# Attention with two gated layers on one core: the planner's transfer rate set to 290 GB/s instead of 265, and all work ordered anew

## The chip, the core and the metric

The kernel runs on one core of a Trainium2 chip. A core has five instruction queues: PE (TensorE, matmuls and transposes; its weight loads are listed as PEld), DVE (VectorE), ACT (ScalarE), POOL (GpSimd) and SP (SyncE), which here issues all the transfers between memory and the on-chip buffers. Each engine works through its own instructions strictly in order and waits on semaphores for what others have to deliver. The metric is device time in microseconds (us), the median of several executions. The profile is of one execution.

## The reference, cut to what matters

```
scores = q @ k.T / 8                       # 4 batches, 8 heads, 576 tokens, head size 64
keep, in each row of 576, the 32 largest; softmax over them; out = attn @ v
x = out as [2304 tokens, 512]
x = (silu(x @ wg) * (x @ wv)) @ wo         # first gated layer, width 1536
x = (sigmoid(x @ wg2) * (x @ wv2)) @ wo2   # second gated layer, other weights
```

All of it in float32. The weights arrive from the host as 64-bit words.

## The kernel before, in words

**Chunks.** The 2304 tokens (36 tiles of 64) are cut into six chunks of 4, 5, 6, 7, 7 and 7 tiles, called chunk 0 to chunk 5. For each chunk the program states attention first and then both layers.

**Attention.** For a pair tile (two times 64 query rows of two heads) PE makes scores in PSUM (`ps_s`, L685 or L668), ACT copies them to `s` (L695, L702; four buffers). DVE finds the 32nd largest of each row with four MAX8 (L875) and three MATCH_REPLACE (L877) for each half of the tile. ACT then makes the exponentials (L835, L839), a reciprocal is taken on DVE (L850), the row is normed into `p` on POOL or ACT (L857, L855), PE transposes it (`ps_t`, L917), ACT copies it to `pt` (L923) and PE multiplies with `v` (`ps_v`, L936).

**Weights.** There are 36 slabs of weights, each of two halves. In chunk 0 each of the 72 halves is loaded as 64-bit words into `wr` (512 KB, three buffers), decoded to float32 by three operations on ACT and POOL (L518 or L520, L532, L541 or L543) and a fourth on DVE (`f4`, L546), which writes the buffer `wf`. From `wf` PE multiplies at once in float32 (L977, operands `xn` and `hn`), and SP stores `wf` to memory as `sw` (256 KB, L550). The chunks 1 to 5 load `sw` again into `raw` (256 KB), split it into a high and a low part (`w`: L498 or L500 for the high one, L503 on POOL for the low one) and do three matmuls for one.

**Layers.** A block of the first product is one `ps_m` tile: four matmuls in chunk 0, twelve in the others. ACT takes the tanh (L1012), DVE multiplies (L948, L952), ACT and POOL split the result into `hh` and `hl`.

**Early scores.** Eight pair tiles of chunk 5 are scored while chunk 0 runs, into `se`, and stored to memory as `ss` (L624). They are loaded again much later (L815).

**What sets the order.** Nothing is issued as stated above. Every piece of work is an `op` with an engine, or a choice of engines, a planned length, what it depends on, which buffers it takes, and a priority. `Plan.run` plays the work through on planned times: whenever an engine is free it takes the ready op of the lowest priority number, and the order in which ops were taken becomes the order of instructions on every engine. A transfer is planned as if one line carried them all, one after another, for `n_bytes / 265.0` ns each, and its data are there 2010 ns (`DMA_LAT`) later. The numbers in the tables at the head of the file (`P_...`, `D_...`, `N...`, one number for each chunk or one for all) are the priorities: `D_WR` of the `wr` loads, `D_ST` of the `sw` stores, `D_RAW` of the `raw` loads, `P_ROUND` of the search for the 32nd largest. `E_SKIP`, `E_IN` and `E_STEP` say between which other ops the early scores are stated.

Of the kernel before, what the change touches and what calls it, by code (L numbers as in the profile page):

```python
# [11 lines left out]
I32 = mybir.dt.int32  # L12
# [5 lines left out]
ALU = mybir.AluOpType  # L18

P = 128  # L20
# [20 lines left out]
EARLY = '000002'  # L41
E_FIRST = 0
E_STEP = 1
E_SKIP = 3
E_LAST = 1
E_IN = [0, 0, 0, 0, 0, 0]
WR = 3
E_PRIO = 0
E_DMA = 2.5
WU = 3  # L50
KE = 2
HP = 3
DL = 6
NA = [0, 2, 2, 2, 2.5, 3]
NP = [1, 1, 0, 0, 2, 0]
P_XC = [0, 1, 0.5, 1, 0, 1]
P_EV = [1, 1, 1, 1, 1, 1]
D_WR = 13
D_ST = 5
D_RAW = [6, 4, 1.0, 2.5, 2.0, 2.5]  # L60
D_K = [0, 1, 1, 3, 0, 1]
D_V = [2.5, 0.5, 4.5, 2.5, 1.5, 2.5]
P_ROUND = [4, 4, 6, 4, 4, 2]
P_MASK = [3, 2, 2, 2, 1, 1]
P_DEC = 2
P_MM = [5, 4.5, 7, 5.5, 6, 6]
P_QK = [0, 1, 3.5, 1.5, 1.0, 3.5]
P_K = [1, 1, 1, 1.5, 1, 5]
P_PT = [2.5, 3.5, 2.5, 2.5, 2.5, 5.5]
P_PV = [1, 1, 0, 2, 0, 0]  # L70
P_EX = [1.5, 3.5, 1.5, 1.5, 0, 0]
P_S = [0.5, 0, 1, 0, 0, 0]
P_X = [1, 0.5, 0, 0, 1.5, 0]
P_HH = [0.5, 1, 2.5, 0.5, 1.0, 2.0]
P_HL = [2, 1.5, 0, 2, 4, 2]
PT = 1
WF = 16
XF = 8
# [15 lines left out]
DEBUG = False  # L94
F1 = {"act": (609, 2), "pool": (700, 2)}
F2 = {"act": (609, 2)}
F3 = {"act": (650, 2), "pool": (810, 2)}
LO = 0
TURN = 2
# [34 lines left out]
class Plan:  # L134
# [5 lines left out]
    def op(self, eng, dur, fn, deps=(), uses=(), allocs=(), prio=0, table=None, lat=DMA_LAT, lock=False):  # L140
        o = Op()
        o.lock = lock
        o.alts = dict(eng) if isinstance(eng, dict) else {eng: (dur, prio)}
        o.eng, o.fn, o.table, o.lat = None, fn, table, lat
        o.deps = [d for d in deps if d is not None]
        o.uses = list(uses) + list(allocs)
        o.allocs = list(allocs)
        o.seq = len(self.ops)
        for g in o.uses:
            g.users += 1  # L150
        self.ops.append(o)
        return o
# [165 lines left out]
def dve(n):  # L318
    return 69 + n / 0.96
# [12 lines left out]


def dma(n_bytes):
    return n_bytes / 265.0


@with_exitstack
def attn_moe_kernel(ctx: ExitStack, tc, qT, kT, qD, kD, vL, wall, outT):
    nc = tc.nc  # L340
    ctx.enter_context(tc.manual_schedule())
    plan = Plan()
    op = plan.op
# [166 lines left out]
    def decode(i, x, prio):  # L510
        r, f, u = new(("wr", 0)), new(("wf", 0)), new(("wu", 0))
        ld = load(r, wall[2 * i + x].bitcast(I32).rearrange("p (a b) -> p a b", b=2),
                  n_bytes=128 * 4096, prio=D_WR)
# [28 lines left out]
            else:  # L542
                nc.gpsimd.tensor_scalar(o, b, 1.0 / 32, -31.0 / 64, op0=ALU.mult, op1=ALU.add)  # L543

        def f4():
            nc.vector.scalar_tensor_tensor(out=f[:].bitcast(I32), in0=f[:].bitcast(I32), scalar=3, in1=u[:],  # L546
                                           op0=ALU.logical_shift_left, op1=ALU.bitwise_or)

        def st():
            nc.sync.dma_start(scr32[i][:, x], f[:])  # L550
        a = op(F1, 0, f1, deps=[ld], uses=[r], allocs=[f])
        b = op(F2, 0, sign, deps=[ld], uses=[r], allocs=[u])
        d = op(F3, 0, f3, deps=[ld], uses=[r], allocs=[u])
        b = op("dve", dve(512) + 30, f4, deps=[a, b, d], uses=[f, u], prio=prio, lock=True)
        stored[i].append(op("dma", dma(128 * 2048), st, deps=[b], uses=[f], prio=D_ST, lat=DMA_LAT))
        return f, b

# [204 lines left out]
    def segment(c, p, b, q0, n_s, x32g, col, held=None):  # L762
# [55 lines left out]
    def row_tile(sg, stg, a, e, pg):  # L818
# [341 lines left out]
```

## Time and profile before

| | us |
|---|---|
| median of 3 runs | 1262.02 |
| lowest and highest of them | 1261.18, 1265.14 |
| the profiled execution, its own time | 1263.24 |
| its span, first to last instruction | 1261.5 |
| PE busy | 1214.4 |
| DVE busy | 881.5 |
| ACT busy | 871.3 |
| POOL busy | 963.9 |

Busy time of PE is the time in which it has at least one matmul under way; ends of matmuls are modelled, so two starts that follow each other tell more than a duration. In the table of stretches below, a row has the stretch in us from the span's start, its length, the busy time of each engine with the number of its instructions in brackets, the granted clock of TensorE as a share of 2.4 GHz, the mean busy share of the 16 DMA engines, and the rate that they moved in GB/s.

### The profile page before, as it was taken

How to read it: one execution, taken by the hardware profiler on the slowest of the kernel's cores; microseconds unless marked ns; L12 is line 12 of the kernel's file. 1: busy time of each engine (PE TensorE's matmuls, PEld its weight loads, DVE VectorE, ACT ScalarE, POOL GpSimd, SP SyncE). 2: the span in 40 equal slices, each digit the busy share in tenths (PEclk: the TensorE clock that was granted, in tenths of full speed). 3: DMA queues.
4: the chain of work that ended last, by engine and by line, in shares of the span. 5: the costliest groups of instructions: out<-in, count | busy, mean ns of one | idle time of the engine just before them, and what ended most of it. 6: DMA issues, size and time to landing. Idle time of an engine off the chain costs nothing.

```text
span 1261.5 us, 21915 instructions
## 1 busy us (share of the span) xinstructions
PE 1214.4 (96%) x7304; PEld 1064.8 (84%) x7304; DVE 881.5 (70%) x1916; ACT 871.3 (69%) x1906; POOL 963.9 (76%) x1030
## 2 busy tenths in 40 slices
PE   5699999989999999999999999999999999999998
PEld 1366867778999899999999898999888899999998
DVE  7999999983999989889989799931949310121110
ACT  5789888876999898788999886344877532332331
POOL 3434455569999999989897887898796587897883
PEclk9699999999999999999999999999999999999999
DMA  7877887876554464544554456335232232433331
GB/s 245 267 249 256 259 267 253 260 260 200 156 170 129 130 197 125 160 138 134 158 156 133 128 178 188 122 101 170 73 111 68 85 104 97 146 117 113 104 104 43
DMA packets 100914, 200.38 MB, mean 159 GB/s; under 512 B 12480, under 2 KB 22848, under 8 KB 100800
## 3 DMA queue, kind: packets, MB, share of 16 engines
q1 hardware_dynamic: 100800, 198.98, 49.5%
q8 instruction: 57, 0.93, 0.3%
q14 instruction: 57, 0.47, 0.1%
HBM read 171.21 MB, written 27.72 MB: 158 GB/s over the span
## 4 chain that ended last, share of the span: by engine, by line
PE 62%; DVE 11%; ACT 4%; DMA 3%; POOL 2%; issue 1%; SPq 0%; POOLq 0%; ACTq 0%; DVEq 0%
PE ps_m L977 52%; DVE st L875 5%; DVE wk L877 4%; PE ps_v L936 4%; PE ps_t L917 3%; PE ps_s L668 3%; DMA wr<-in_wall_dram 1%; DMA raw<-sw 1%; POOL w L503 1%; ACT w L498 1%; ACT p L839 1%; ACT e L835 1%; DVE h L948 1%; ACT s L695 0%; DVE wf L546 0%
## 5 line engine op out<-in xcount | busy, mean ns | idle before, releaser
L503 POOL TENSOR_TENSOR w<-raw,w 128x512 fp32r<-128x512 f32 x360 | 465.4, 1310 | 10.5 <-ACT w L498 3.3
L977 PE MATMUL ps_m<-xh,w 128*128 128x448 f32 (+2 forms) x1920 | 398.4, 349 | 0.3 <-DVE sil L948 0.3
L977 PEld LDWEIGHTS ps_m<-xh,w 128*128 128x128 f32 x1920 | 336.6, 188 | 16.2 <-issue 1.3
L875 DVE MAX8 st<-wk 128x8 f32<-128x576 f32 x432 | 315.0, 748 | 1.0
L977 PE MATMUL ps_m<-xl,w 128*128 128x448 f32 (+2 forms) x960 | 215.6, 346 | 0.0
L877 DVE MATCH_REPLACE8 wk<-st,wk 128x576 f32<-128x576 f32 x288 | 213.1, 742 | 0.0
L977 PE MATMUL ps_m<-hh,w 128*128 128x448 f32 (+2 forms) x960 | 200.5, 350 | 0.0
L977 PEld LDWEIGHTS ps_m<-xl,w 128*128 128x128 f32 x960 | 172.1, 188 | 7.1
L977 PEld LDWEIGHTS ps_m<-hh,w 128*128 128x128 f32 x960 | 168.8, 188 | 8.1
L498 ACT ACTIVATE w<-raw 128x512 fp32r<-128x512 f32 x249 | 151.5, 624 | 20.5 <-PE ps_m L977 8.4
L503 POOL TENSOR_TENSOR hl<-h,hh 128x448 fp32r<-128x448 f32 (+2 forms) x120 | 128.7, 1074 | 8.3 <-ACT hh L498 5.1
L875 DVE MAX8 st<-s 128x8 f32<-128x576 f32 x144 | 105.1, 747 | 32.3 <-ACT s L695 31.7
L948 DVE SCALAR_TENSOR_TENSOR sil<-sil,ps_m 128x448 f32<-128x448 f32 (+3 forms) x84 | 41.0, 489 | 123.1 <-ACT sil L1012 123.0
L498 ACT ACTIVATE hh<-h 128x448 fp32r<-128x448 f32 (+2 forms) x113 | 61.1, 542 | 93.2 <-DVE h L948 66.3
L835 ACT ACTIVATE e<-s,st 128x576 f32<-128x576 f32 x144 | 109.8, 769 | 16.5 <-DVE st L875 15.6
L923 ACT ACTIVATE pt<-ps_t 128x512 f32<-128x512 f32 (+4 forms) x288 | 112.8, 418 | 11.2 <-PE ps_t L917 9.7
L917 PE MATMUL ps_t<-ident,p 128*128 128x128 f32 x656 | 102.6, 283 | 14.8 <-POOL p L857 6.6
L948 DVE SCALAR_TENSOR_TENSOR h<-sil,ps_m 128x448 f32<-128x448 f32 (+2 forms) x60 | 34.4, 574 | 117.0 <-PE ps_m L977 113.5
L500 POOL TENSOR_SCALAR w<-raw 128x512 fp32r<-128x512 f32 x111 | 69.2, 625 | 57.1 <-PE ps_m L977 56.3
L917 PEld LDWEIGHTS ps_t<-ident,p 128*128 128x128 f32 x656 | 77.8, 143 | 40.8 <-POOL p L857 14.3
L839 ACT ACTIVATE p<-e,st 128x576 f32<-128x576 f32 x144 | 110.4, 768 | 1.7 <-PE ps_t L917 0.8
L1012 ACT ACTIVATE sil<-ps_m 128x448 f32<-128x448 f32 (+4 forms) x156 | 71.7, 459 | 56.7 <-PE ps_m L977 56.2
(64 smaller groups left out, 1812.3 us busy)
## 6 DMA issues: line engine op xcount, KB each, us to landing
raw<-sw SPq DMA_DIRECT2D x360, 256.0 KB, 3.0
wr<-in_wall_dram SPq DMA_DIRECT2D x72, 512.0 KB, 4.6
sw<-wf SPq DMA_DIRECT2D x72, 256.0 KB, 2.7
kr<-in_kD_dram SPq DMA_DIRECT2D x42, 288.0 KB, 3.0
v<-in_vL_dram SPq DMA_DIRECT2D x34, 320.0 KB, 3.9
ss<-se SPq DMA_DIRECT2D x6, 576.0 KB, 2.9
s<-ss SPq DMA_DIRECT2D x6, 576.0 KB, 5.2
k<-in_kT_dram SPq DMA_DIRECT2D x11, 288.0 KB, 4.4
```

What stands on the lines that cost most here:

```text
L498: nc.scalar.activation(out=hi(), in_=raw(), func=AF.Copy)
L500: nc.gpsimd.tensor_scalar(hi(), raw(), 1.0, 1.0, op0=ALU.mult, op1=ALU.mult)
L503: (nc.gpsimd if eng == "pool" else nc.vector).tensor_sub(lo(), (lo_raw or raw)(), lo_hi() if lo_hi else f32(hi()))
L835: nc.scalar.activation(out=eg[:], in_=src(), func=AF.Prelu, bias=stg[:, 31:32], scale=-1.0, alpha=1.0 / STEEP)
L839: nc.scalar.activation(out=pg[:, e * S:(e + 1) * S], in_=eg[:], func=AF.Exp, bias=stg[:, 32:33], scale=-STEEP, accum_out=stg[:, 33:34])
L875: nc.vector.max(out=stg[:, 4 * k:4 * k + 8], in_=src() if k == 0 else fresh[:])
L877: nc.vector.match_replace(out=fresh[:], in_to_replace=stg[:, 4 * k - 4:4 * k + 4], in_values=src() if k == 1 else fresh[:], imm_value=NEG)
L917: nc.tensor.transpose(tg[:width, i], pg[:, a:a + width], ident)
L923: nc.scalar.activation(out=dst(), in_=src(), func=AF.Copy)
L948: nc.vector.scalar_tensor_tensor(out=out, in0=t, scalar=1.0, in1=x, op0=ALU.add, op1=ALU.mult)
L977: nc.tensor.matmul(pg[:, :n], blk(a, d), src(x, d), start=first and i == 0, stop=last and i == 4 * len(terms) - 1)
L1012: nc.scalar.activation(out=sg[:, :n], in_=pg[:, :n], func=AF.Tanh, scale=0.5)
```

## The change

The planned rate of a transfer goes from 265 to 290 GB/s, and 17 of the constants and tables at the head are set to other numbers. Two of them move where the early scores are stated: they now begin inside chunk 0's attention. `f4` gets a table of engines of its own; it names DVE alone, with the same length and priority as before, so the branch for POOL in it is never taken. A small tile `eight` is filled once by POOL.

```diff
-E_SKIP = 3
+E_SKIP = 4
-E_IN = [0, 0, 0, 0, 0, 0]
+E_IN = [2, 0, 2, 0, 0, 0]
...
-D_WR = 13
-D_ST = 5
+D_WR = 12.5
+D_ST = 4
...
+F4 = {"dve": (632, 2)}
...
 def dma(n_bytes):
-    return n_bytes / 265.0
+    return n_bytes / 290.0
...
+    eight = pool("eight", 1).tile([P, 1], I32, tag="eight", name="eight")
+    nc.gpsimd.memset(eight, 8)
...
-        def f4():
+        def f4(eng):
...
-        b = op("dve", dve(512) + 30, f4, deps=[a, b, d], uses=[f, u], prio=prio, lock=True)
+        b = op(F4, 0, f4, deps=[a, b, d], uses=[f, u], lock=True)
```

The same instructions remain, apart from the choice between ACT and POOL for some of them; the order of all five queues is new. Lines stand up to seven further down in the changed file: L491 is L494 there, L546 is L551, L550 is L557, L624 is L631, and behind these all are seven further (L875 is L882, L977 is L984). A number at the end of a name is only the order in which buffers were made.

First place: DVE, behind the 55th of the 72 decodes and up to the 57th (`wf` is a decode; `st`, `wk` and `s` belong to the search). Before:

```order
L877 MATCH_REPLACE wk_2477<-st_2468,wk_2477 128x576
L877 MATCH_REPLACE wk_2509<-st_2473,wk_2509 128x576
L875 MAX st_2468<-wk_2477 128x8
L875 MAX st_2473<-wk_2509 128x8
L546 SCALAR_TENSOR_TENSOR wf_2556<-wf_2556,wu_334 128x512
L877 MATCH_REPLACE wk_2509<-st_2473,wk_2509 128x576
L875 MAX st_2592<-s_2223 128x8
L875 MAX st_2473<-wk_2509 128x8
L850 RECIPROCAL st_2468<-st_2468 128x1
L877 MATCH_REPLACE wk_2607<-st_2592,s_2223 128x576
L948 SCALAR_TENSOR_TENSOR hn_2244<-sil_2596,ps_m_2586 128x256
L546 SCALAR_TENSOR_TENSOR wf_2594<-wf_2594,wu_355 128x512
```

In the changed kernel, the same two decodes:

```order
L882 MAX st_2353<-wk_2372 128x8
L882 MAX st_2446<-s_2161 128x8
L884 MATCH_REPLACE wk_2372<-st_2353,wk_2372 128x576
L884 MATCH_REPLACE wk_2458<-st_2446,s_2161 128x576
L955 SCALAR_TENSOR_TENSOR hn_2185<-sil_2448,ps_m_2437 128x256
L551 SCALAR_TENSOR_TENSOR wf_2444<-wf_2444,wu_319 128x512
L551 SCALAR_TENSOR_TENSOR wf_2462<-wf_2462,wu_351 128x512
```

Eight instructions of the search stood before these two decodes, and four stand there now. Ahead of the last decode there are 166 MAX, 124 MATCH_REPLACE and 40 reciprocals in the order before, and 153, 114 and 36 in the new one.

Second place: SP, the first stores of early scores (`ss`) among loads (`wr`, `v`) and stores of weights (`sw`). Before:

```order
L550 DMA sw_67<-wf_688 128x512
L491 DMA wr_750<-in_wall_dram 128x1024
L624 DMA ss_0_2_195<-se_734 128x1152
L550 DMA sw_68<-wf_722 128x512
L550 DMA sw_68<-wf_740 128x512
L624 DMA ss_0_4_196<-se_784 128x1152
```

In the changed kernel:

```order
L494 DMA wr_462<-in_wall_dram 128x1024
L557 DMA sw_65<-wf_449 128x512
L631 DMA ss_0_2_200<-se_464 128x1152
L494 DMA v_520<-in_vL_dram 128x640
L494 DMA wr_530<-in_wall_dram 128x1024
L631 DMA ss_0_4_201<-se_517 128x1152
```

The first store stood behind the 15th load of `wr` and now stands behind the 8th. All eight such stores now stand ahead of the 19th load of `wr`, where before it was four.

Third place: PE, where chunk 0 ends and chunk 1 begins (`hn`,`wf`: chunk 0; `xh`, `xl`, `w`: chunk 1). Before:

```order
L917 MATMUL ps_t_3050<-ident,p_2967 128x128
L977 MATMUL ps_m_3025<-hn_2244,wf_3021 128x256 x4
L977 MATMUL ps_m_3025<-hn_2244,wf_3047 128x256 x4
L917 MATMUL ps_t_3091<-ident,p_3057 128x128 x4
L977 MATMUL ps_m_3099<-xh_1882,w_3064 128x320 x4
L977 MATMUL ps_m_3099<-xh_1882,w_3066 128x320 x4
L977 MATMUL ps_m_3099<-xl_1883,w_3064 128x320 x4
L977 MATMUL ps_m_3127<-xh_1882,w_3065 128x320 x4
L977 MATMUL ps_m_3127<-xh_1882,w_3067 128x320 x4
L977 MATMUL ps_m_3127<-xl_1883,w_3065 128x320 x4
```

In the changed kernel:

```order
L984 MATMUL ps_m_3035<-hn_2185,wf_2891 128x256 x4
L984 MATMUL ps_m_3075<-xh_1924,w_2904 128x320 x4
L984 MATMUL ps_m_3075<-xh_1924,w_2906 128x320 x4
L984 MATMUL ps_m_3075<-xl_1925,w_2904 128x320 x4
L984 MATMUL ps_m_3104<-xh_1924,w_2905 128x320 x4
L984 MATMUL ps_m_3104<-xh_1924,w_2907 128x320 x4
L984 MATMUL ps_m_3104<-xl_1925,w_2905 128x320 x4
L924 MATMUL ps_t_3129<-ident,p_3093 128x128 x4
L984 MATMUL ps_m_3035<-hn_2185,wf_2937 128x256 x4
L924 MATMUL ps_t_3184<-ident,p_3093 128x128 x4
L924 MATMUL ps_t_3193<-ident,p_3093 128x128
```

The four matmuls on the last decoded half (`wf_3047`, now `wf_2937`) stood ahead of chunk 1's first block. Two blocks of chunk 1 now stand ahead of them.

## Rows read from the trace of the kernel before

**Rows 1.** The page, busy time of PE over the span.
```profile
PE 1214.4 (96%) x7304; PEld 1064.8 (84%) x7304; DVE 881.5 (70%) x1916; ACT 871.3 (69%) x1906; POOL 963.9 (76%) x1030
```

**Rows 2.** Busy time by stretch; columns as told above.
```profile
32.00:256.00 224.00, 204.00 (x1447) 147.86 (x1446) 221.91 (x499) 193.18 (x427) 106.74 (x155) 0.93 0.80 260
256.00:320.00 64.00, 58.79 (x348) 51.65 (x347) 40.13 (x85) 45.13 (x95) 51.88 (x53) 0.97 0.70 222
320.00:559.00 239.00, 236.96 (x1585) 222.20 (x1584) 221.47 (x493) 211.28 (x493) 223.53 (x219) 1.00 0.49 150
```

**Rows 3.** The chain that ended last, two long pieces: start us, us, what.
```profile
241.08 4.68 DMA wr<-in_wall_dram
...
997.14 174.27 PE ps_m L977 x867
```

**Rows 4.** Longest wait of DVE in 32 to 256 us: sum, times, longest.
```profile
DVE wf L546 <- ACT wu L532: 0.6, 1, 0.6
```

**Rows 5.** DVE in order of time, 214 to 236 us: start us, us, what.
```profile
213.92 1.39 DVE L875 MAX8 st<-s 128x8 f32<-128x576 f32 x2
215.24 0.07 DVE L877 MATCH_VALUE_LOAD wk<-st,s 128x8 f32 x1
...
217.56 0.07 DVE L877 MATCH_VALUE_LOAD wk<-st,s 128x8 f32 x1
...
218.28 0.07 DVE L877 MATCH_VALUE_LOAD wk<-st,wk 128x8 f32 x1
...
220.28 0.14 DVE L850 RECIPROCAL st<-st 128x1 f32<-128x1 f32 x1
220.34 0.73 DVE L875 MAX8 st<-wk 128x8 f32<-128x576 f32 x1
```

**Rows 6.** Tile wr, 120 to 276 us: count, ns min/median/max, first and last start.
```profile
L491 SPq DMA_DIRECT2D wr<-in_wall_dram x46: 327/358/1903, 119.7 to 268.1; - x46
L543 POOL TENSOR_SCALAR wu<-wr x41: 770/782/1337, 121.9 to 273.7; 128x512 uint8<-128x512 uint8 x41
L520 POOL TENSOR_SCALAR wf<-wr x29: 651/670/1266, 125.9 to 273.0; 128x512 f32<-128x512 f32 x29
...
DMA to landing us min/median/max: 3.5/4.5/6.6
```

**Rows 7.** The 32 us with the most moved between 64 and 256 us.
```profile
160.00:192.00 32.00, 31.14 (x183) 21.89 (x177) 31.91 (x69) 28.23 (x64) 19.21 (x26) 1.00 0.85 267
```

**Rows 8.** The 8 us with the most moved in that stretch.
```profile
112.00:120.00 8.00, 7.03 (x73) 5.05 (x76) 8.00 (x19) 7.59 (x19) 3.86 (x5) 1.00 0.90 304
```

**Rows 9.** Tile wf, 120 to 276 us, its decodes on DVE; columns as for tile wr.
```profile
L546 DVE SCALAR_TENSOR_TENSOR wf<-wf,wu x48: 668/684/1141, 124.3 to 275.6; 128x512 int32<-128x512 int32 x48
```

**Rows 10.** PE in order of time, 274 to 292 us.
```profile
275.04 3.72 PE L977 MATMUL ps_m<-hn,wf 128*128 128x256 f32 x16 [0.38 <-DVE wf L546]
278.60 0.60 PE L917 MATMUL ps_t<-ident,p 128*128 128x128 f32 x4
278.96 1.42 PE L977 MATMUL ps_m<-xh,w 128*128 128x320 f32 x8
...
282.56 1.33 PE L977 MATMUL ps_m<-xh,w 128*128 128x320 f32 x8
```

**Rows 11.** Waits of DVE in 256 to 320 us, the longest in sum.
```profile
DVE sil L948 <- ACT sil L1012: 15.7, 8, 4.5
```

**Rows 12.** PE in order of time, 554 to 564 us, around chunk 2's second layer.
```profile
555.02 0.29 PE L668 MATMUL ps_s<-kh,qs 128*128 128x288 f32 x1
555.15 0.29 PE L668 MATMUL ps_s<-kl,qs 128*128 128x288 f32 x1
...
555.63 1.85 PE L936 MATMUL ps_v<-pt,v 128*64 128x192 f32 x20
...
558.83 1.63 PE L977 MATMUL ps_m<-xh,w 128*128 128x384 f32 x8
```

**Rows 13.** Busy time and count of the MAX instructions (L875), 0 to 559 us.
```profile
0.00:559.00 559.00, 240.81 (x337) 0.97 0.65 207
```

More of the change, by code (lines that the diff above doesn't have):

```diff
@@ L51 @@
 KE = 2
-HP = 3
+HP = 3.5
 DL = 6
 NA = [0, 2, 2, 2, 2.5, 3]
-NP = [1, 1, 0, 0, 2, 0]
-P_XC = [0, 1, 0.5, 1, 0, 1]
-P_EV = [1, 1, 1, 1, 1, 1]
-D_WR = 13
-D_ST = 5
-D_RAW = [6, 4, 1.0, 2.5, 2.0, 2.5]
+NP = [1, 1, 2, 3.5, 4, 2]
+P_XC = [0, 1, 2.5, 3, 2, 3]
+P_EV = [0.5, 1, 1, 1, 1, 1]
+D_WR = 12.5
+D_ST = 4
+D_RAW = [6, 4, 0, 1.5, 1.0, 1.5]
 D_K = [0, 1, 1, 3, 0, 1]
 D_V = [2.5, 0.5, 4.5, 2.5, 1.5, 2.5]
-P_ROUND = [4, 4, 6, 4, 4, 2]
-P_MASK = [3, 2, 2, 2, 1, 1]
-P_DEC = 2
+P_ROUND = [3, 3.5, 6, 4, 4, 4]
+P_MASK = [3, 2, 2, 0, 1, 1]
+P_DEC = 3.5
 P_MM = [5, 4.5, 7, 5.5, 6, 6]
@@ L70 @@
 P_PV = [1, 1, 0, 2, 0, 0]
[L71 to L75, printed above, removed]
+P_EX = [1.5, 3.5, 0.5, 2.5, 1, 1]
+P_S = [0.5, 2.5, 1, 0, 1, 0]
+P_X = [1, 0.5, 1, 1, 2.5, 1]
+P_HH = [0.5, 1, 3.5, 0, 0, 2.0]
+P_HL = [3, 1.5, 0, 2.5, 4, 2]
 PT = 1
@@ L543, in f3 @@
                 nc.gpsimd.tensor_scalar(o, b, 1.0 / 32, -31.0 / 64, op0=ALU.mult, op1=ALU.add)
-        def f4():
-            nc.vector.scalar_tensor_tensor(out=f[:].bitcast(I32), in0=f[:].bitcast(I32), scalar=3, in1=u[:],
-                                           op0=ALU.logical_shift_left, op1=ALU.bitwise_or)
+        def f4(eng):
+            w = f[:].bitcast(I32)
+            if eng == "dve":
+                nc.vector.scalar_tensor_tensor(out=w, in0=w, scalar=3, in1=u[:], op0=ALU.logical_shift_left, op1=ALU.bitwise_or)
+            else:
+                nc.gpsimd.tensor_tensor(out=w, in0=w, in1=eight[:].to_broadcast([P, 512]), op=ALU.mult)
+                nc.gpsimd.tensor_tensor(out=w, in0=w, in1=u[:], op=ALU.add)
         def st():
```

## The prediction

> **What bounds the kernel now.** I read the busy times first. PE is busy for 96% of the span [rows 1], which looks like a kernel that only fewer matmuls could shorten. The stretches say something else [rows 2]. From 320 us on PE is busy 237 of 239 us. From 32 to 256 us DVE is the full one, 222 of 224 us, and ends of matmuls are modelled, so PE's busy time there hides waiting. The chain of waits agrees [rows 3]: in the first part loads of weights stand in it among DVE's work, one of 4.7 us at 241, and at the end it is matmuls alone, one piece of 174 us. So there are two parts. The first ends when chunk 0's last weights are decoded, and it can be made shorter by the order alone. In the second PE has a fixed load, and an order can only spoil it.
>
> In the first part DVE's longest wait is 0.6 us [rows 4], so it sets the pace, and transfers follow it: DVE decodes a half, that frees the store to `sw`, the next load of `wr` stands behind that store in SP's order. The granted clock is 0.93 in this stretch [rows 2], most of it at the higher of the two levels, 2.4 GHz; while DVE sets the pace, the part at 1.2 GHz costs nothing that a row shows.
>
> **What the change does to the first part.** The orders hold the same 72 decodes, but 13 MAX, 10 MATCH_REPLACE and 4 reciprocals fewer stand ahead of the last one. From start to start, two MAX take 1.32 us (213.92 to 215.24), so 0.66 each; a MATCH_REPLACE with its load takes 0.72 (217.56 to 218.28); a reciprocal 0.06 [rows 5]. That is 13 x 0.66 + 10 x 0.72 + 4 x 0.06 = 16.0 us less on the engine that sets the pace. So the last decode can come up to 16 us earlier, if transfers allow it.
>
> Do they? I added up sizes in SP's order: 69.0 MB were issued ahead of the last `wr` load, and 69.4 are now. That load was issued at 268.1 us [rows 6], so the mean was 257 GB/s. All 16 us earlier means 69.4 MB in 252.1 us, 275 GB/s. The best of the 32 us stretches from 64 us on moved 267 [rows 7]; single 8 us reached 304, at a share of 0.90 [rows 8]. At 267 the last load goes out at 69.4 MB / 267 = 260 us, 8 us earlier.
>
> The loop of buffers gives the same middle. 46 loads went out from 119.7 to 268.1 us, one each 3.30 us, and with three buffers one turn is 9.9 us. A turn needs 4.5 us from issue to landing, 0.67 + 0.78 on POOL (ACT's operation lies beside them) [rows 6], 0.7 for the decode on DVE [rows 9], and two issues on SP of about 0.35 [rows 6]: 7.3 us. So 2.6 us of a turn are waiting. Taking 16.0 / 72 = 0.22 us from each decode shortens a turn by 0.7, which fits only if landings don't lengthen. I take 8 of the 16, with 0 and 16 as the ends, and a little below 0 if landings lengthen much.
>
> Here the Trainium skill speaks against the change. The rows show landings from 3.5 to 6.6 us in one stretch [rows 6], while the planner gives each load its planned time and 2.01 us, 3.82 us at 290. The Trainium skill ("DMA: Bandwidth & Descriptors", Latency and other measured facts) puts the access time of memory at 0.2 us on average and 2 us at high load; by that the fixed part grows as more is moved, and the 8 would shrink toward 0. The spread in the rows agrees in kind; no row tells it from transfers that share the engines.
>
> The early stores of scores now all stand ahead of the 18th load. Their bytes are in the 69.4 MB, so they are paid in the mean rate.
>
> **Where chunk 1 begins.** After the last decode PE still did four matmuls of chunk 0, a transpose and two blocks of chunk 1 (278.96 to 282.56, 3.6 us) before the third block [rows 10]. Those two blocks now stand ahead of the last four matmuls, so PE does them while it waits. One more group of transposes falls behind the decode, some 0.5 us. That is worth 0 to 3.1 us, by whether their weights are split in time; I take 2.5.
>
> **What is given back.** What was taken from before the last decode has to be done later. In 256 to 320 us DVE is busy 40.1 of 64 us [rows 2], and its largest wait there is for ACT's part of the products, 15.7 us [rows 11]: it has little else in its order. The 16 us of search fit into this hole.
>
> Beyond it the new order wants more. I take the first block of chunk 2's second layer, started at 558.8 us [rows 12]. Ahead of it PE now has 9 more score pieces (four matmuls of 0.13 us [rows 12]), 17 more groups of transposes (0.36 for four [rows 10]) and 3 more products with `v` (some 1.8 us [rows 12]): 4.7 + 6 + 5.4 = 16 us. DVE has to be done with 34 MAX, 26 MATCH_REPLACE and 11 reciprocals more: 22.4 + 18.7 + 0.7 = 41.8 us. It was idle 41.4 us from 256 to 559 (23.9 + 17.5 [rows 2]), and PE's extra work lends it 16. It also was ahead: 337 MAX had begun by 559 us [rows 13], and PE needed those up to the 329th in DVE's order; 8 MAX and their 4 or 5 MATCH_REPLACE are 8 us. So 41.4 + 16 + 8 - 41.8 = 23.6 us remain for DVE's new waits and PE's gain together. Of these, 8 are the waits of the first part (the half of the 16 that doesn't arrive). Up to this point the gain is therefore at most 15.6 us less what DVE waits between 256 and 559. In full stretches it hardly waits, but the hole is filled only in part: 24 - 16 = 8, and I add 1.6. That leaves 6 us of the 10.5 gained; 4.5 are given back. POOL is busy 223.5 of 239 us there too [rows 2] and has little room either, another reason to give something back.
>
> **The sum.** 8 + 2.5 - 4.5 = 6.0 us. The profiled execution took 1263.24 us, of which 1261.5 is the span; 1263.2 - 6.0 = 1257.2. That execution is 1.2 us above the median of 1262.02. I predict 1257. A difference under 0.3%, some 3.8 us, can't be told from no change.
>
> **Rivals.**
>
> *The transfers hold the full pace.* For it: 304 GB/s in 8 us at a share of 0.90 [rows 8], so there is room above 275. Against it: no 32 us did it. Price: the full 16, 2.5 more, 4 back: 1263.2 - 14.5 = 1249. The Trainium skill (the same page, Where 436 GB/s comes from) has 358 GB/s as a core's limit to memory; by that 69.4 MB take 194 us, transfers never bind, and this rival is the outcome. No row of this case comes near that rate.
>
> *The transfers go no faster.* The turn of three buffers stays 9.9 us because landings lengthen as loads are asked for sooner. For it: landings already reach 6.6 us [rows 6], and the planner counts 3.82. Then DVE waits for `wr` instead of searching, the first part gives 0, the reordered blocks 2.5, and 3 are given back: 1264. If landings lengthen by more than the 2.6 us of waiting in a turn can take up, each of the 24 turns adds what is over; I price this end at 4 us, 0.17 a turn, 1268.
>
> *DVE becomes the bound in chunk 2, and the kernel is slower.* The same account decides it: once DVE waits more than 15.6 us between 256 and 559 us, the first block of chunk 2's second layer comes later than before, and what comes after it on PE is the same work. For it: it waited 41.4 there, and new scores for it come only when PE reaches them behind chunk 1's first blocks. Against it: its waits were in a stretch where little stood in its order. With 22 us of waiting, PE loses 6: 1263.2 + 6 = 1269.
>
> **How the numbers follow.** The forecast, with half of the first part's gain kept, 0.42 (1252 to 1261; a quarter of it is inside 0.3%); full pace 0.18; no faster 0.20 (1261 to 1268: 0.12 the same, 0.08 slower); DVE the bound 0.20 (0.06 the same, 0.14 slower). Faster: 0.32 + 0.18 = 0.50. The same: 0.10 + 0.12 + 0.06 = 0.28. Slower: 0.08 + 0.14 = 0.22. Cases of both signs are open, so the range goes from 1248, just below full pace, to 1268, the worse end of the third case; the likeliest case by itself has 1252 to 1261.
>
> **What the new profile would show.** If the steps hold: the last DVE decode starts near 267 us instead of 275.6 [rows 9]; the rate from 32 to 256 us rises from 260 [rows 2] to about 267 GB/s; DVE shows waits before `wf` of some 8 us in sum, where the longest was 0.6; the idle time of DVE from 256 to 320 us falls from 24 to about 10. The second part on PE, from 320 us on, stays as full as it is. The forecast is wrong if the last decode starts at 275 or later (transfers), or if it comes early and PE then shows waits for `p` or `pt` behind DVE's search between 400 and 600 us.

## The result: 0.7% slower, and the profile after

The changed kernel took 1273.4 us (median; 1270.7 to 1275.4) beside 1262.6 for the kernel before: ratio 1.0072, 95% interval [1.0057, 1.0087]. (These two medians are 10.8 us apart, which is the upper end of that interval.) The forecast was 1257, the range 1248 to 1268. Its profiled execution took 1275.4 us, 1273.5 of it the span.

The page's first row and the three stretches that answer to [rows 1, 2]; the columns are those told there:

```profile
PE 1221.8 (96%) x7304; PEld 1065.5 (84%) x7304; DVE 880.6 (69%) x1916; ACT 870.2 (68%) x1903; POOL 962.7 (76%) x1034
```

```profile
32.00:256.00 224.00, 199.78 (x1437) 147.56 (x1438) 216.96 (x484) 186.94 (x411) 114.76 (x161) 0.96 0.81 268
256.00:320.00 64.00, 59.30 (x366) 52.27 (x365) 51.77 (x114) 48.54 (x110) 50.90 (x55) 0.97 0.58 187
320.00:559.00 239.00, 236.85 (x1610) 220.40 (x1608) 235.91 (x529) 225.36 (x517) 218.67 (x227) 1.00 0.49 150
```

The decodes of 120 to 276 us (tile wf) and DVE's waits from 32 to 256 us, answering to [rows 9, 4]:

```profile
L551 DVE SCALAR_TENSOR_TENSOR wf<-wf,wu x48: 668/687/1441, 123.3 to 265.9; 128x512 int32<-128x512 int32 x48
```

```profile
DVE wf L551 <- POOL wu L546: 2.7, 5, 0.7
DVE wf L551 <- POOL st L837: 1.4, 1, 1.4
```

So the transfers did what was forecast: 268 GB/s instead of 260, the last decode 9.7 us earlier (275.6 to 265.9), DVE idle 7.0 of 224 us (5.0 of them ahead of `wf`, where some 8 were expected), and from 256 to 320 us idle 12.2 us instead of 23.9. What PE made of it, in order of time (answering to [rows 10]):

```profile
276.58 0.75 PE L984 MATMUL ps_m<-xl,w 128*128 128x320 f32 x4
280.82 0.81 PE L924 MATMUL ps_t<-ident,p 128*128 128x128 f32 x4 [3.49 <-POOL p L864]
281.42 3.46 PE L984 MATMUL ps_m<-hn,wf 128*128 128x256 f32 x8
```

The matmuls on the last decoded half begin at 281.4 us, 15 us after their decode: PE stood 3.5 us ahead of them, for a row of `p`. DVE's search for that row was over at 274.9 us, 2.4 us before PE's wait began. ACT came to its exponential (`e`) only at 277.2, since it first waited 2.9 us for a load of `raw` and then split weights:

```profile
275.31 1.32 ACT L501 ACTIVATE w<-raw 128x512 fp32r<-128x512 f32 x2 [2.92 <-DMA raw<-sw]
...
277.21 0.76 ACT L842 ACTIVATE e<-s,st 128x576 f32<-128x576 f32 x1
```

So the postponed search explains at most a part of this wait.

The bigger loss is in the second part, which I had taken as fixed. One stretch of 100 us with nothing but matmuls of 448 columns in it, before and after, by busy time and by the instructions on `xl` (ns min/median/max of one):

```profile
1010.00:1110.00 100.00, 100.00 (x500) 93.44 (x499) 12.43 (x20) 32.80 (x60) 85.59 (x80) 1.00 0.36 119
```

```profile
1010.00:1110.00 100.00, 100.00 (x489) 91.50 (x488) 10.57 (x17) 32.20 (x59) 83.39 (x78) 1.00 0.34 115
```

```profile
L977 PE MATMUL ps_m<-xl,w x119: 360/363/363, 1010.8 to 1109.9; 128*128 128x448 f32 x119
```

```profile
L984 PE MATMUL ps_m<-xl,w x116: 365/367/370, 1010.6 to 1109.6; 128*128 128x448 f32 x116
```

PE is 100.00 us busy in both, at a granted clock of 1.00, but 500 matmuls became 489. The same instruction on the same shapes is slower: from start to start 205.5 ns instead of 200.0 on `xl` (mean over its 540 recorded matmuls of 448 columns), 207.6 instead of 202.7 on `xh` (mean over all its 1152, with some longer steps in both), 176.7 instead of 173.4 on `xl` with 384 columns, and the same at 320 columns (146.6, before 146.7).

A table to read this with: the start of a block of matmuls, less all work that stands ahead of it in PE's order, each matmul at its usual spacing in the trace of before. What is left is time in which PE stood or went slower than usual, in us. (Two columns belong to experiments below; in the last one the matmuls that were added count as such time too. Each column is one profiled execution.)

| block | before | after | after without `eight` | last experiment |
|---|---|---|---|---|
| chunk 0, first (70 to 76 us) | 39.9 | 33.5 | 35.6 | 31.8 |
| chunk 0, 29th (124 to 129) | 41.2 | 41.5 | 45.0 | 39.9 |
| chunk 0, second gated layer (181 to 186) | 43.9 | 46.6 | 49.5 | 43.9 |
| chunk 1, first (269 to 279) | 53.3 | 50.9 | 52.7 | 46.4 |
| chunk 1, first layer's product with `wo` (326 to 335) | 57.4 | 57.2 | 56.1 | 49.0 |
| chunk 2, second gated layer (559 to 577) | 66.4 | 68.6 | 67.7 | 60.6 |
| chunk 3, second gated layer (780 to 789) | 73.2 | 76.9 | 75.3 | 67.7 |
| chunk 5, near the end (1214 to 1231) | 77.5 | 89.1 | 80.3 | 72.7 |

Up to chunk 1's product with `wo` the change is neither better nor worse (57.4, 57.2); from there it loses 11.8 us, most of it where both kernels run the same matmuls back to back.

### The profile page after: what moved, and what is told of

It is laid out like the page before. It is cut to its first block, busy times and chain, and to the rows that moved or that the text cites. A ratio compares the mean times of both kernels' runs of the same rounds, so it can differ in the third digit from the quotient of the medians.

```text
span 1273.5 us, 21896 instructions
## 1 busy us (share of the span) xinstructions
PE 1221.8 (96%) x7304; PEld 1065.5 (84%) x7304; DVE 880.6 (69%) x1916; ACT 870.2 (68%) x1903; POOL 962.7 (76%) x1034
## 4 chain that ended last, share of the span: by engine, by line
PE 57%; DVE 8%; ACT 3%; POOL 1%; issue 1%; DMA 0%; DVEq 0%; ACTq 0%; POOLq 0%
PE ps_m L984 49%; DVE st L882 4%; DVE wk L884 3%; PE ps_v L943 3%; PE ps_t L924 3%; PE ps_s L675 2%; ACT w L501 1%; DVE sil L955 0%; DVE h L959 0%; ACT p L862 0%; ACT pt L930 0%; ACT p L846 0%; DMA kr<-in_kD_dram 0%; ACT e L842 0%; POOL w L506 0%
## 5 line engine op out<-in xcount | busy, mean ns | idle before, releaser
L984 PE MATMUL ps_m<-xh,w 128*128 128x448 f32 (+2 forms) x1920 | 405.2, 353 | 0.0
L984 PEld LDWEIGHTS ps_m<-xh,w 128*128 128x128 f32 x1920 | 337.7, 188 | 20.3 <-issue 0.7
L882 DVE MAX8 st<-wk 128x8 f32<-128x576 f32 x432 | 313.4, 748 | 0.7
L984 PE MATMUL ps_m<-xl,w 128*128 128x448 f32 (+2 forms) x960 | 219.2, 350 | 0.0
L984 PE MATMUL ps_m<-hh,w 128*128 128x448 f32 (+2 forms) x960 | 201.6, 352 | 0.0
L984 PEld LDWEIGHTS ps_m<-xl,w 128*128 128x128 f32 x960 | 172.7, 188 | 10.2
L984 PEld LDWEIGHTS ps_m<-hh,w 128*128 128x128 f32 x960 | 168.7, 188 | 10.1 <-issue 0.8
L882 DVE MAX8 st<-s 128x8 f32<-128x576 f32 x144 | 105.8, 747 | 17.3 <-ACT s L702 17.2
L1019 ACT ACTIVATE sil<-ps_m 128x448 f32<-128x448 f32 (+4 forms) x156 | 71.8, 460 | 67.1 <-PE ps_m L984 66.4
L924 PE MATMUL ps_t<-ident,p 128*128 128x128 f32 x656 | 102.0, 281 | 14.5 <-POOL p L864 10.8
L924 PEld LDWEIGHTS ps_t<-ident,p 128*128 128x128 f32 x656 | 77.5, 142 | 39.5 <-POOL p L864 16.6
```

The costliest lines, as they stand in the source:

```text
L882: nc.vector.max(out=stg[:, 4 * k:4 * k + 8], in_=src() if k == 0 else fresh[:])
L924: nc.tensor.transpose(tg[:width, i], pg[:, a:a + width], ident)
L984: nc.tensor.matmul(pg[:, :n], blk(a, d), src(x, d), start=first and i == 0, stop=last and i == 4 * len(terms) - 1)
L1019: nc.scalar.activation(out=sg[:, :n], in_=pg[:, :n], func=AF.Tanh, scale=0.5)
```

## Where the 11 us come from: 32 bytes

The diff adds a tile `eight`, 4 bytes in each partition; no order that the planner chose ever reads it. It takes 32 bytes, and each tile opened behind it lies 32 bytes higher: `xh` at 68320 instead of 68288, `xl` at 75488 instead of 75456, `hh` and `hl` as well. The weights `w`, opened earlier, stay (17024 and steps of 2048). Modulo 128 bytes the moving operands were 64 from the weights, and are 96. Theory A: this distance slows the matmuls, and the new order is worth nothing. Theory B: the order does it.

The new order at the old addresses:

```diff
-    eight = pool("eight", 1).tile([P, 1], I32, tag="eight", name="eight")
-    nc.gpsimd.memset(eight, 8)
...
```

> The changed kernel without the tile `eight` (and without the branch that would read it, which is never taken): the order of all work stays the new one, `xh`, `xl`, `hh`, `hl` lie 32 bytes lower, at the addresses they had before. Theory A (the 32-byte shift makes PE's 448-column and 384-column matmuls slower, the new order itself is worth about nothing): 1259 to 1265 us, ratio to before 0.998 to 1.002; the 448-column matmuls on xh start 200 to 201 ns apart on average, as before, and not 205; in a full stretch of chunk 5 100 us hold 499 recorded matmuls again, not 489. Theory B (the new order costs the 11 us, because DVE, POOL or the transfers run beside PE's matmuls at other times): 1271 to 1275, ratio 1.006 to 1.009, 205 ns.

Measured: 1263.7 us beside 1263.6, ratio 1.0003 [0.9992, 1.0013], and 500 matmuls in the stretch:

```profile
1010.00:1110.00 100.00, 100.00 (x500) 93.44 (x499) 12.28 (x20) 33.43 (x61) 85.98 (x80) 1.00 0.37 119
```

The old order with the tile:

```diff
+    eight = pool("eight", 1).tile([P, 1], I32, tag="eight", name="eight")
+    nc.gpsimd.memset(eight, 8)
```

> The kernel before with only the tile `eight` and its one memset added: old order, everything behind the tile 32 bytes higher. Theory A (shift): 1272 to 1276 us, ratio 1.008 to 1.011, 205 ns from start to start of the 448-column matmuls on xh, 203.4 on hh. Theory B (order): 1261 to 1264, ratio 0.999 to 1.001, 200 ns.

Measured: 1273.0 beside 1263.6, ratio 1.0071 [1.0058, 1.0084], the whole slowdown without any change of order, and the same 489:

```profile
1010.00:1110.00 100.00, 100.00 (x489) 91.52 (x488) 11.81 (x19) 31.81 (x59) 82.63 (x79) 1.00 0.36 115
```

Which tile is it? First only raw, `xh` and `xl` moved, then only what lies behind them. (In the two expectations "first layers" are the products on `xh` and `xl`, "second layers" those with `wo` on `hh` and `hl`.)

```diff
-    pool("pad", 1).tile([P, 16], F32, tag="pad", name="pad")
+    pool("pad", 1).tile([P, 24], F32, tag="pad", name="pad")
     arena = pool("arena", 1)
-    pool("pad2", 1).tile([P, 16], F32, tag="pad2", name="pad2")
+    pool("pad2", 1).tile([P, 8], F32, tag="pad2", name="pad2")
```

> The kernel before with one unused tile 32 bytes longer and the next one 32 bytes shorter: only the tiles between them (raw, `xh`, `xl`) move by 32 bytes, `hh`, `hl` and all else stay. Theory A (the place of the moving operand): the first layers' 448-column matmuls go to 205 ns, the second layers' stay at 202; about three quarters of the 11 us, 1268 to 1273, ratio 1.005 to 1.008. If the place of another shifted tile (scores, masks, the float32 output) is what counts, 1261 to 1264 and 200 ns. Theory B: 1261 to 1264.

```diff
-    pool("pad2", 1).tile([P, 16], F32, tag="pad2", name="pad2")
+    pool("pad2", 1).tile([P, 24], F32, tag="pad2", name="pad2")
```

> The kernel before with the second unused tile 32 bytes longer: raw, `xh`, `xl` stay, all that lies behind them (scores, masks, the float32 output, `hh`, `hl`) moves by 32 bytes. By the theory that the place of the moving operand counts: only the second layers' 448-column matmuls slow down, hh from 202 to 204 ns, the first layers stay at 200; 288 matmuls on hh and hl a chunk in three chunks by 1.5 to 2 ns and a part of chunk 2: 1.3 to 2 us, 1264 to 1266, ratio 1.001 to 1.002. If the place of another shifted tile had a part in the 9.4 us of the kernel with all tiles shifted: 1266 or more.

Measured: 1271.6, ratio 1.0062 [1.0050, 1.0074], and 1264.4, ratio 1.0007 [0.9999, 1.0016]; 8.0 and 0.9 us, together nearly the 9.4 of all tiles (the 0.9 by itself is not clear of noise). The stretch of 1010 to 1110 us by groups (count, busy us, mean ns of one) shows that each shift slows only its own operand. First the kernel before, then the first shift, which slows `xl`, then the second, which slows `hh`:

```profile
L977 PE MATMUL ps_m<-xl,w 128*128 128x448 f32 x119 | 28.7, 362 | 0.0
L977 PE MATMUL ps_m<-hh,w 128*128 128x448 f32 x96 | 21.4, 364 | 0.0
```

```profile
L977 PE MATMUL ps_m<-xl,w 128*128 128x448 f32 x116 | 28.5, 367 | 0.0
L977 PE MATMUL ps_m<-hh,w 128*128 128x448 f32 x96 | 21.4, 364 | 0.0
```

```profile
L977 PE MATMUL ps_m<-xl,w 128*128 128x448 f32 x117 | 28.2, 361 | 0.0
L977 PE MATMUL ps_m<-hh,w 128*128 128x448 f32 x96 | 21.6, 366 | 0.0
```

Which places are bad? The tile at 64 bytes (distance 0), a shift by 96 (distance 32), and the weights shifted along by 64 (distance 64 as before, all places other):

```diff
-    eight = pool("eight", 1).tile([P, 1], I32, tag="eight", name="eight")
+    eight = pool("eight", 1).tile([P, 16], I32, tag="eight", name="eight")
```

> The changed kernel with `eight` 64 bytes long a partition instead of 4: new order, the moving operands 64 bytes above their old place instead of 32. Theory A in its narrow form (what counts is whether the operand starts on a multiple of 64 bytes): as the kernel without the tile, 1259 to 1265, 200 to 201 ns. Theory A in a wide form (any other place than the old one is worse, or a neighbour of these tiles is to blame): 1271 to 1275. Theory B (order): 1271 to 1275, 205 ns.

```diff
-    pool("pad", 1).tile([P, 16], F32, tag="pad", name="pad")
+    pool("pad", 1).tile([P, 40], F32, tag="pad", name="pad")
```

> The kernel before with the first unused tile 96 bytes longer: old order, moving operands at 32 modulo 128 instead of 64 (the changed kernel had 96, the one with 64 bytes more had 0). If any start other than 64 modulo 128 costs: 1267 to 1276, 203.5 to 206 ns on xl. If only places past the 64th byte cost: 1262 to 1265, 200 ns.

```diff
+    pool("pad0", 1).tile([P, 16], F32, tag="pad0", name="pad0")
     home_pool = pool("home", 1)
```

> The kernel before with a 64-byte tile ahead of the weights' tiles, so that the weights `w` and the moving operands `xh`, `xl`, `hh`, `hl` all move by 64 bytes and keep their distance. Theory R (the distance of moving operand and weights modulo 128 bytes counts): as before, 1262 to 1265, 200 ns on xl. Theory M (the place of the moving operand by itself counts): as with the moving operands moved alone by 64 bytes, 1267 to 1272, 204 ns on xl.

| moving operand from weights, modulo 128 | time over before, us | `xl`, start to start, ns |
|---|---|---|
| 64 (before) | 0 | 200.0 |
| 96 (`eight`; old order) | +9.4 | 205.4 |
| 0 (64 bytes; new order) | +6.0 | 204.0 |
| 32 (96 bytes; old order) | +7.2 | 203.7 |
| 64, all moved by 64 | -0.6, ratio 0.9998 [0.9989, 1.0007] | 200.0 |

It is the distance that counts and not the address: theory R. My narrow form (a multiple of 64 is good) fell with the third row; the wide form's range missed it too (1269.6 beside 1271 to 1275). That the period is 128 bytes is the simplest reading and no more: modulo 256 `xl` was tried at 64, 96, 128 and 160 alone, and only 64 is good. `hh` and `hl` lie 192 away modulo 256 in the kernel before, which is 64 modulo 128, and fit: the matmuls on `hh` have 202.3 ns there (steps under 260 ns), and 204.1 to 205.1 in the second to fourth row. By the spacings over all records of the old order with the tile, the slower matmuls sum to 12 us, while the time shows 9.4; where the rest is hidden I can't place. The Trainium skill ("SBUF — State Buffer", Operand start alignment) asks only that an operand start at a multiple of its element size, which all five rows do. It calls this a matter of legality and not of speed, and gives no price for a place; the table above shows one.

## What the order is worth: nothing, and why

Without the 32 bytes the new order gives 0.0 us instead of the 6.0 forecast. First its two halves apart, at the old addresses: the rate alone, and the tables alone.

```diff
-    return n_bytes / 265.0
+    return n_bytes / 290.0
```

> The kernel before with 290 in place of 265 GB/s in the planner and every number of the tables as before; all tiles at their old places. Theory A (an order can win little in the first part, because PE there waits only 7 us in sum from 150 to 300 us in both orders): 1260 to 1267, ratio 0.998 to 1.003, last decode between 266 and 276 us. Rival (the numbers of the tables take back what the rate gives): 1254 to 1258, last decode near 266.

```diff
-    return n_bytes / 290.0
+    return n_bytes / 265.0
```

> New tables without the tile `eight`, with transfers planned at 265 GB/s as before. Theory (rate and tables are one fit: the rate alone cost 9 us, both together nothing): the tables alone are also worse than the pair, 1266 to 1273, with more waits of PE in the first 70 us than the 35.6 us of the pair. Rival (the tables are better by themselves, the rate only harms): 1252 to 1259.

Measured: 1272.9, ratio 1.0075 [1.0061, 1.0089], and 1271.1, ratio 1.0065 [1.0052, 1.0079]. For the rate alone both theories were wrong. Rate and tables are a pair: each costs 8 to 9 us alone, and together they cost nothing. The waits of PE up to 150 us (sum, times, longest) say what each lacks. The rate alone has its last decode at 268.5 us, and PE waits for `s` (12.6 before); the tables alone have it at 277.7, and PE waits for weights:

```profile
PE ps_s L685 <- ACT s L695: 20.7, 16, 4.5
```

```profile
PE ps_m L979 <- DVE wf L549: 6.6, 5, 2.8
```

So an early last decode by itself brings no good time: the rate alone has it 7 us earlier than the kernel before and is 9.4 us slower. What sets the first part's pace? Three cuts in the new order: PE's work (in 16 blocks of the first products of the second gated layer, called there the second experts, two of four matmuls are left out), DVE's work (the search of chunks 0 and 1 leaves out half of the scores), both.

```diff
-                for d in range(4):
+                for d in range(nd):
...
-                            mms(pg, blk, lambda x, d: xs[x][:, d, o:o + n], n, True, True)
+                            mms(pg, blk, lambda x, d: xs[x][:, d, o:o + n], n, True, True,
+                                2 if c == 0 and moe_i == 1 and f < 8 else 4)
...
```

> New order without the tile `eight`; in chunk 0's second experts' first layer, in 8 of 12 weight groups, only half of the products' terms are summed (two of four matmuls), so PE has 16 x 0.86 = 13.8 us less to do between 186 and 240 us; every decode, load and search stays. Theory P (in the first part PE's own work sets the pace: it waited 7.2 us in sum from 150 to 300 us): 8 to 13 us less than 1263.7, 1251 to 1256. Theory D (DVE sets it: its search hardly pauses up to 280 us, and PE then waits for `p` that DVE's search is late for): PE only waits longer, 0 to 4 us less, 1260 to 1264.

```diff
-        last, m0 = top_full(sg, src, stg, a)
+        last, m0 = top_full(sg, src, stg, a, 288 if now[0] < 2 else S)
...
-                    nc.vector.max(out=stg[:, 4 * k:4 * k + 8], in_=src() if k == 0 else fresh[:])
+                    nc.vector.max(out=stg[:, 4 * k:4 * k + 8], in_=(src() if k == 0 else fresh[:])[:, :w])
...
```

> New order without the tile `eight`; in chunks 0 and 1 MAX and MATCH_REPLACE go over 288 of the 576 scores (the threshold comes from half of them), so DVE has about 282 x 0.3 = 85 us less to do before 280 us; PE's work and the order stay. Theory D (DVE sets the first part's pace): 10 us less or more, 1245 to 1254. Theory P (PE's own work sets it, and the 7.2 us of waits are all there is to win): 3 to 7 us less, 1257 to 1261.

> New order without the tile `eight`, with both cuts at once: two of four matmuls left out in 16 blocks of chunk 0 (13.8 us of PE's work), and the search of chunks 0 and 1 over half of the scores (some 85 us of DVE's). The cuts alone gave 2.2 and 4.9 us. Theory of a balanced first part (PE's own work and DVE's search end together, so either cut alone only uncovers the other): together far more than their sum of 7, 14 to 20 us less than 1263.7, 1244 to 1250. Rival (transfers or POOL bound the first part behind both): no more than the sum, 1255 to 1260.

Measured: 1261.5, ratio 0.9991 [0.9979, 1.0002]; 1258.8, ratio 0.9962 [0.9948, 0.9975]; 1253.7, ratio 0.9933 [0.9914, 0.9952]; by medians 2.0 (not clear of noise), 4.7 and 9.3 us less than the kernel before on the same chip. Each single cut came out as the other theory wanted it, so neither P (PE's work sets the pace) nor D (DVE's does) holds. With 13.8 us less work PE's waits from 150 to 300 us grow from 7.2 to 18.5 us (four of five rows shown); 11 of the 13.8 turned into waiting. First the two largest of the new order without `eight`, then those of the cut:

```profile
PE ps_t L919 <- POOL p L859: 3.5, 4, 2.3
PE ps_s L687 <- ACT s L697: 2.3, 3, 1.1
```

```profile
PE ps_t L919 <- POOL p L859: 6.4, 7, 1.4
PE ps_s L687 <- ACT s L697: 6.3, 6, 1.9
PE ps_s L687 <- ACT s L704: 2.9, 2, 1.4
PE ps_t L919 <- ACT p L857: 2.7, 3, 2.0
```

With half the search DVE is busy 162 of 224 us and PE still gains only 4.7:

```profile
32.00:256.00 224.00, 201.83 (x1462) 149.62 (x1463) 162.37 (x497) 191.92 (x425) 113.67 (x164) 0.98 0.82 275
```

Both cuts together give more than their sum of 6.7 (by a difference that the intervals don't clear of noise), but less than the 14 to 20 of a balance of PE and DVE alone; neither theory's range holds the result. Its profile has a granted clock of 0.95 from 150 to 280 us, where each single cut has 1.00:

```profile
150.00:280.00 130.00, 121.12 (x671) 89.37 (x671) 104.92 (x272) 111.80 (x253) 84.27 (x108) 0.95 0.84 276
```

Between the levels of 2.4 and 1.2 GHz a mean of 0.95 is 13 us at half speed, 6.5 us lost at most. That pointed to a term I had left out.

## The granted clock

In the kernel before, the clock is low from 30 to 70 us, where PE waits anyway, and 1.00 from 70 to 130. In the new order without `eight` it is better in the first and worse in the second, where PE is nearly full:

```profile
30.00:70.00 40.00, 27.39 (x193) 15.33 (x190) 38.83 (x82) 32.67 (x66) 17.62 (x29) 0.62 0.76 257
70.00:130.00 60.00, 57.00 (x535) 42.94 (x534) 59.59 (x144) 53.79 (x125) 23.18 (x36) 1.00 0.76 256
```

```profile
30.00:70.00 40.00, 29.02 (x224) 13.60 (x224) 37.65 (x83) 34.68 (x68) 13.93 (x27) 0.81 0.79 270
70.00:130.00 60.00, 53.93 (x467) 43.09 (x468) 56.87 (x136) 46.93 (x109) 26.95 (x39) 0.90 0.72 238
```

In order of time, what PE did before the clock fell in the latter: it waited 1.2 us twice, and a score piece of the same size then took 1.24 us instead of 0.72:

```profile
62.46 0.72 PE L687 MATMUL ps_s<-ke,qe 64*64 64x288 f32 x8 [1.24 <-ACT se L697]
64.38 0.72 PE L687 MATMUL ps_s<-ke,qe 64*64 64x288 f32 x8 [1.20 <-ACT se L697]
65.10 1.12 PE L919 MATMUL ps_t<-ident,p 128*128 128x128 f32 x5
66.16 1.24 PE L687 MATMUL ps_s<-k,q 64*64 64x288 f32 x8
```

The table above agrees: without `eight` the new order is 4.3 us ahead at its first block and 3.8 behind by the 29th. The Trainium skill ("TensorE: Matmul & The Clock Gate", HAM oscillation) describes a matmul engine that waits between batches, falls back to the slow clock and starts the next batch slow; these rows agree in kind, with shorter waits (1.2 us each) than in its example, and for ACT instead of transfers.

Theory K, the clock takes the gain, was tested by giving PE matmuls that need nothing while it waits. First behind the score pieces:

```diff
+                fill[0] += 1
+                if fill[0] <= 44:
+                    for h in [0, 1] * 2:
+                        r = slice(64 * h, 64 * h + 64)
+                        nc.tensor.matmul(psg[64 * h:64 * h + 64, h, 288:], qg[r, o * 64:o * 64 + 64], kg[r, :224],
+                                         start=True, stop=True)
```

> New order without the tile `eight`; behind each of the first 44 score pieces PE does four more matmuls of 224 columns into columns of the same PSUM tile that nobody reads, so that it works where it waited for ACT to empty the tile. Theory K (the order's gain of 4 us up to 70 us is lost from 70 to 130 us, where the granted clock falls behind waits and PE is busy again at half speed): the granted clock from 70 to 130 us rises from 0.91 to 0.98 or more, 5 us of PE's time come back, 1 to 3 us go to fills that no wait covers: 2 to 4 us less than 1263.7, 1259.5 to 1262. Rival (the clock is no cause, waits for `s` set the pace there): no gain, 1263.5 to 1267, whatever the clock shows.

The same with `[0, 1] * 4`:

> The same with eight more matmuls behind each of the first 44 score pieces instead of four. Theory K: the clock at 0.98 or more as well, but some 0.5 us more in each piece, more than most waits hold: 1261 to 1268. Rival: 1268 to 1275.

The first of these edits in the kernel before:

> The kernel before with the same four matmuls behind each of the first 44 score pieces. Its granted clock is low only from 36 to 70 us, where PE waits in any case, and 1.00 from 70 to 260 us. Theory K: nothing to win, 1262 to 1266, ratio 0.999 to 1.002. Rival (filling waits helps by itself, whatever the clock): as much as in the new order.

Measured: 1275.5 (1.0097 [1.0080, 1.0114]), 1298.7 (1.0277 [1.0260, 1.0294]) and 1284.3 (1.0166 [1.0148, 1.0183]); all three expectations missed. The clock did rise, to 1.00 from 30 to 130 us in the new order, but in this program ACT empties a PSUM tile only behind the last matmul into it, so the wait came again behind the fill:

```profile
52.31 0.71 PE L689 MATMUL ps_s<-ke,qe 64*64 64x288 f32 x8 [0.74 <-ACT s L705]
52.85 0.94 PE L695 MATMUL ps_s<-ke,qe 64*64 64x224 f32 x8
54.52 0.72 PE L689 MATMUL ps_s<-ke,qe 64*64 64x288 f32 x8 [0.74 <-ACT se L705]
```

So 44 fills cost their full time, 23.2 us by the step from four to eight. If the first four cost as much, they gave 11 back in the new order (+11.8 instead of +23.2) and 2 in the old (+20.8). That is a difference of differences, and the price was not measured in the old order; so fills were put ahead of the waiting instructions instead, into a PSUM tile that nobody reads:

```diff
+    def fill(i, table, to=None):
+        n = table.get(seen[i], 0)
+        seen[i] += 1
+        if n:
+            fl = R["ps_t"].make(f"fl_{seen[i]}") if to is None else to
+            for _ in range(n):
+                nc.tensor.matmul(fl[:, 0, :64], ident[:], ident[:, :64], start=True, stop=True)
...
```

> New order without the tile `eight`; small matmuls of 64 columns on the identity, into a PSUM tile that nobody reads, stand ahead of those 13 score pieces and 4 groups of transposes from 30 to 120 us at which PE waited 0.3 us or more, 3 to 16 of them (0.9 of each wait at 0.13 us each), so that PE works while it waits and ACT isn't held up. Theory K (the new order loses its early gain to a granted clock that falls behind these waits): the clock from 70 to 130 us rises from 0.90 to 0.97 or more and 4 to 9 us come back: 1255 to 1260. Rival (the clock takes nothing; the fills of four a piece cost what they cost for another reason): 1262 to 1267.

> The kernel before with the same, ahead of its own 6 score pieces and 5 groups of transposes at which PE waited from 30 to 120 us. Its granted clock is low at 30 to 70 us only, and low clocks there fall into waits: 0 to 3 us less, 1260 to 1264, even if the clock there rises from 0.62 to 0.9. Rival (the low clock costs there as much as in the new order): 1254 to 1259.

Measured: 1274.2 (1.0084 [1.0070, 1.0097]) and 1272.3 (1.0064 [1.0050, 1.0077]). Both missed their ranges and tell nothing of K: one such matmul (two records in the trace) took some 0.23 us at the higher clock and 0.48 at the lower one, not 0.13, so the fills outlasted the waits (2.40 us for five, ahead of a wait of 0.78), two of them waited for ACT themselves, and the clock from 70 to 130 us stayed at 0.91 in the new order and fell to 0.94 in the old:

```profile
31.59 2.40 PE L487 MATMUL fl<-ident 128*128 128x64 f32 x10
...
75.90 1.91 PE L487 MATMUL fl<-ident 128*128 128x64 f32 x10 [2.35 <-ACT pt L939]
```

The last one has fills that fit (its edit is shown against the one just above, in the new order):

```diff
-FILL_QK = {10: 3, 11: 5, 14: 8, 16: 6, 17: 6, 20: 6, 21: 4, 24: 8, 25: 10, 27: 5, 28: 6, 36: 5, 39: 16}
-FILL_TR = {4: 3, 9: 5, 16: 5, 18: 6}
+FILL_QK = {11: 2, 14: 3, 16: 3, 17: 3, 24: 4, 25: 4, 28: 3, 36: 2, 39: 8}
+FILL_TR = {4: 1, 9: 2, 16: 2, 18: 3}
-                nc.tensor.matmul(fl[:, 0, :64], ident[:], ident[:, :64], start=True, stop=True)
+                nc.tensor.matmul(fl[:, 0], ident[:], ident[:], start=True, stop=True)
```

> New order without the tile `eight`; matmuls of 128 columns on the identity (0.27 us each) into a PSUM tile that nobody reads, ahead of 9 score pieces and 4 groups of transposes at which PE waited, so many that they take 0.9 of the wait, and none where the fill itself would wait. Theory K: the granted clock from 70 to 130 us rises from 0.90 to 0.97 or more, 3 to 7 us come back, 1257 to 1261. Rival (the clock takes nothing): the clock rises and the time stays, 1263 to 1266. If the clock doesn't rise, the run tells neither.

Measured: 1259.7 us beside 1263.5, ratio 0.9975 [0.9965, 0.9986]: faster than the kernel before and 13.7 us faster than the changed one. The clock rose as K wanted, and the time fell by 4.0 from the 1263.7 of the new order without `eight` (measured on another chip; the kernel before took 1263.6 there and 1263.5 here):

```profile
30.00:70.00 40.00, 33.86 (x291) 19.70 (x293) 38.56 (x83) 34.35 (x69) 14.82 (x27) 0.91 0.79 274
70.00:130.00 60.00, 56.33 (x525) 46.39 (x521) 59.60 (x145) 48.91 (x113) 29.91 (x41) 1.00 0.77 258
```

K's rival, that the clock takes nothing, is out, and K holds with one correction: by the table half of the gain is there at the first block (35.6 to 31.8), in the stretch of 30 to 70 us, and the loss up to the 29th block only shrinks from 9.4 to 8.1, since some 4 us of fills there take the place of waits. The table's two executions lie 7.6 us apart and the medians 4.0, so its sizes are rough. Fitting fills in the old order were not tried, so what the low clock costs there is open.

## Why the prediction was wrong, step by step

- **Transfers: right.** 8 us was forecast for the last decode, 9.7 came; 267 GB/s was forecast, 268 came. The rival of no faster transfers is out, and so is full pace (the 16 us).
- **"PE's busy time there hides waiting": the step that failed for the order.** I set 8 us of earlier decode equal to 8 us of earlier PE. From 150 to 300 us PE had waited 3.8 us for decodes in the trace of before, and 7.0 in all; the earlier decode could give no more. In the new order the 3.8 are gone, and in the changed kernel 7.2 us of waits for `p` stand there. The postponed search explains little of them: in the two longest, 2.5 us at 174.9 and the 3.5 at 277.3, it was over 6.2 and 2.4 us before the wait began, and ACT and POOL came to the row late:

```profile
PE ps_m L977 <- DVE wf L546: 3.8, 2, 3.4
PE ps_t L917 <- ACT p L855: 1.2, 2, 0.7
```

```profile
PE ps_t L924 <- POOL p L864: 7.2, 5, 3.5
PE ps_s L692 <- ACT s L702: 2.2, 3, 1.2
```

  By the cuts neither DVE's work nor PE's sets the pace alone, so "it sets the pace", said of DVE, was at best half of it; what else binds there was not shown.
- **The reordered blocks, 2.5: not seen.** The transposes in front of the last decode's matmuls waited 3.5 us (3.49 in the changed kernel; 2.30 without `eight`).
- **The part at the lower clock "costs nothing that a row shows": wrong.** For the kernel before it was not tested; in the new order the last experiment wins 4.0 us with a higher clock.
- **Given back, 4.5: near in size, the reason not shown.** In the table the new order without `eight` is 1.3 us ahead at chunk 1's first product with `wo` and 2.8 behind at the end, 4.1 given back. But its profiled execution was 2.4 us above its median, so the agreement can be luck. DVE's account held in the hole: 12.2 us idle where some 10 were forecast. DVE did not become the bound: from 400 to 600 us PE waited 1.0 us for `p` and `pt` in the changed kernel and 0.9 in the one before, so this sign of being wrong did not come.
- **The second part "stays as full as it is": true and misleading, and the step that failed for the time.** Its busy share stayed, its matmuls grew slower. The tile `eight` was given no price, since no instruction of it is on a path. It costs 9.4 us in the old order and 9.7 in the new (there between medians from two chips); this term alone puts the result on the other side of no change. All my rivals on the slow side were about waits, and the one with its own account, DVE as the bound at 1269, didn't happen.
- **The sum and the range.** 1257 was counted from the profiled execution (1263.2), while the result goes by medians, 1.2 us lower; from there the same terms give 1256. The range ended at 1268, below the 1269 of a rival that had a chance of 0.20. Neither changes the outcome.

## What to carry to other kernels

An unused tile is a change of layout: look at where the operands of the hottest instruction lie before and after, and read instructions per 100 us, not the busy share, to see whether the engine runs as fast. What an earlier producer can give is at most what its consumer waited for it; read that sum first, and then which wait takes its place. Where PE waits in small pieces, look at the granted clock of the full stretch behind them; matmuls that need nothing and fit into the wait can pay for themselves.

## What the runs showed of the hardware

- On `xl`, matmuls of 448 and 384 columns in this float32 form run 200.0 and 173.4 ns from start to start where the moving operand lies 64 bytes from the weights modulo 128, and 203.7 to 205.5 and up to 176.7 where it lies 0, 32 or 96 away. At 320 columns (146.6 to 146.7) nothing is seen of it. Which part of the chip does this, no run shows.
- Neither the operand's own address nor a multiple of 64 decides: weights and moving operands moved by 64 bytes together gave 200.0 ns and ratio 0.9998, the moving operands moved by 64 alone 204.0 ns.
- The granted clock fell to the lower level behind waits of 1.2 us that followed each other (a score piece then took 1.24 us instead of 0.72), and stayed at 1.00 from 70 to 130 us where matmuls stood in such waits.
- In this program ACT's emptying of a PSUM tile waited for all matmuls into the tile ahead of it in the order, also those into columns that it doesn't read (0.74 us of PE's waiting for each of two fills above). That the chip asks for this, no run shows.
